# A three-layer kernel: seven block products for eight in the last layer's first matmul, a variance moved to ScalarE, and a new order of the last stage

## The chip, the cores and the metric

The kernel runs on one core of one Trainium2 chip. The metric is the device time of one execution, in microseconds (us). TensorE (PE in the profile; PEld is its weight load), VectorE (DVE), ScalarE (ACT), GpSimd (POOL) and SyncE (SP, which issues nearly all DMAs) run side by side. Each works through its own instructions strictly in order, and waits on semaphores for the others.

## The reference, cut to what matters

Attention with a decay feeds a feed-forward layer, and that feeds a second layer with a softmax gate and a layer norm. The change lies in the second layer, so this is the part to know:

```python
# 4 batches x 576 positions = 2304 tokens, 8 heads x 64 = 512 channels
x = attention(q, k, v, f)                        # (2304, 512)
y = leaky_relu(x @ w_in) @ w_out                 # first layer, 512 -> 2048 -> 512
h = y @ w2_in                                    # second layer's first product, 512 -> 1024
e = exp(h - max(h)); sm = e / (sum(e) + 1e-9)    # per token
s = h * sm
ln = (s - mean(s)) / sqrt(var(s) + 1e-6) * g_ln
out = ln @ w2_out                                # second layer's second product, 1024 -> 512
```

## The kernel before, in words

**Numbers.** Every float32 operand of a large product is scaled by a power of two and split into a high and a low float16 half. A product is then three float16 matmuls, high by high, high by low and low by high, summed in PSUM. `split` does this for a weight tile (`copy_f` writes the high half, `sub_f` the low one), `load_y` for the first layer's result. The scale comes from the largest value of the block: `bound` takes row maxima, and `power` sends them through a small float32 matmul against `ident` to spread the maximum over the partitions. That small matmul stands in PE's queue like any other.

**Stages.** Attention and the first layer (`ffn`: units of one 256-token block by one half of the hidden width) are interleaved until about 413 us. Then come the rest of the `ffn` units, and from 563 us the second layer. The 2304 tokens are 9 blocks of 256, taken in the order of the table `ORDER`. `load_y` reads a block of the first layer's result back from DRAM and splits it. A block is two tiles of 128 tokens, and `layer2` works on one tile.

**One tile of the second layer.** PE makes h: 128 tokens by 1024 columns in one of two PSUM tiles `ph` of two banks, 24 matmuls of 512 columns (two halves by four slices of 128 channels by three). DVE takes the row maximum (line 1083) and scales it (1085). ACT makes the exponential and its row sum (1086). DVE takes the reciprocal (1089, 1091) and multiplies gate and h (1092), after which `ph` is free. DVE takes mean and variance (1097, 1098), POOL the reciprocal root (1103 to 1106), and DVE applies both (1109). The result is split again (`hl`, lines 475 and 487), a DMA transposes it into `tr`, and PE makes the output tile: 24 matmuls of 512 columns into a bank `ps_g` or `ps_f`. ACT moves it to `ot` (1129), and a DMA writes it out.

**What sets the order.** The program isn't written in the order in which it runs. Each step is handed to a planner, `Plan`, with an engine (or a choice of engines), an estimated duration, a priority and the buffers that it touches. `Plan.run` plays the steps through against these estimates and emits each as its engine and buffers come free; the order of the instructions on every engine is fixed there, when the kernel is built. `prio` is the order wanted (lower first), `copy_f` and `sub_f` leave the engine to the planner, and `heirs` passes a tile on to another use once its first one has ended. So the three banks `ps_f` of the first layer go to `ps_g` after the last `ffn` unit; until then `ps_g` is a single bank.

All matmuls are recorded under line 518, the line of their helper `mm`. The profile's other helper lines are 472 to 479 (copies), 483 to 487 (differences), 658 (row maxima), 676 to 681 (`power`) and 781 (`tensor_tensor_reduce`, which adds two tensors and takes a row maximum or minimum in one instruction; here in attention).

Of the kernel before, what the change touches and what calls it, by code (L numbers as in the profile page):

```python
# [10 lines left out]
I32 = mybir.dt.int32  # L11
# [19 lines left out]
ORDER = (0, 1, 4, 5, 3, 2, 6, 8, 7)  # L31
# [11 lines left out]
EP = 1367.16  # L43
# [16 lines left out]
NWY = 19  # L60
NY2 = 4
NHL2 = 1
# [3 lines left out]
YB_ENGS = ("ACT",)  # L66
# [10 lines left out]
US0 = 20.0  # L77
HST = 2.59
# [41 lines left out]
WEIGHT2 = {"DVE": 0.71}  # L120
# [13 lines left out]
LO_ENGS = ("DVE", "POOL")  # L134

# [264 lines left out]
def body(tc, kqa, kq, vt, f, wa, w2i, w2o, gln, out):  # L400
# [80 lines left out]
    def sub_on(eng, o, a, b, scale=None):  # L481
# [5 lines left out]
        (nc.vector if eng == DVE else nc.gpsimd).tensor_tensor(o, a, b, op=ALU.subtract)  # L487
# [13 lines left out]
    def sub_f(o, a, b, n, prio, engs=(DVE, POOL), scale=None, psum=False, **kw):  # L501
        d = {DVE: dve(n) + (60 if scale else 0), POOL: pool2(n) + (pool1(n) + 40 if scale else 0)}
        return flex(engs, [d[e] for e in engs], lambda e: sub_on(e, o(), a(), b(), scale and scale()), prio, lock=not psum, **kw)
# [101 lines left out]
    attn_ops, XB = [], {}  # L605
# [347 lines left out]
    def split_w2i(prio):  # L953
        power(EI, 2 * KD + 1, [(EX, ("i2", j)) for j in range(2 * KD)], EW, "w2", prio, "ps_g")
        inverse(IW, ev(EW), "v2", "w2", prio)
        for h in range(2):
            for k in range(KD):
                W2I[k, h] = P.buf("wz")
                split(ZI[2 * k + h], W2I[k, h], lambda: ev(IW), [(EX, "v2")], prio + 0.3 * k + h)

    def load_w2o(c, prio):
        z, q = whole(w2o[c], prio), P.buf("wz")
        copy_f(lambda: q.t, lambda: z.t, 512, prio, scale=lambda: glt[:, c:c + 1], w=[q], r=[z])
        ZQ[c] = q
        sums(q, EQ + c, prio)
# [79 lines left out]
    def load_y(blk, prio):  # L1045
        yws, ys = [], []
        for q in range(2):
            yw = P.buf("yw")
            load(yw, lambda yw=yw: yw.t.rearrange("p (a n) -> p a n", a=2), lambda q=q: yp_d[blk][:, 2 * q:2 * q + 2], 128 * 512 * 4, prio, deps=YPD[blk][q:q + 1])
            bound(lambda yw=yw: yw.t, 512, EY + 3 * blk + q, ("y2", blk, q), prio, YB_ENGS, r=[yw])  # L1050
            yws.append(yw)
        power(EY + 3 * blk, 3, [(EX, ("y2", blk, q)) for q in range(2)], EE + blk, ("e", blk), prio, "ps_g")
        inverse(IY + blk, ev(EE + blk), ("iy", blk), ("e", blk), prio)
        P.op(DVE, 140, lambda: nc.vector.tensor_scalar(ev(SY + blk), ev(EE + blk), ev(EW), 2.0 ** (-2 * TOP), op0=ALU.mult, op1=ALU.mult), prio,
# [3 lines left out]
        for yw in yws:  # L1058
            y = P.buf("y2")
            copy_f(lambda y=y: y.t[:, 0], lambda yw=yw: yw.t, 512, prio, scale=lambda: ev(IY + blk), w=[(y, 0)], r=[yw, (EX, ("iy", blk))])  # L1060
            sub_f(lambda y=y: y.t[:, 1], lambda yw=yw: yw.t, lambda y=y: y.t[:, 0], 512, prio, scale=lambda: ev(IY + blk), w=[(y, 1)], rw=[yw], r=[(y, 0), (EX, ("iy", blk))])
            ys.append(y)
        return ys

    def layer2(tb, e, ys, prio, oprio):
        tt = 2 * tb + e
        eprio = prio - 5000
        ps, Eb, st, blk = P.buf("ph"), P.buf("raw2"), P.buf("s2"), ORDER[tb]
        E = lambda a=0, b=1024: Eb.t[:, a:b]
# [12 lines left out]
        P.op(PE, 24 * mmr(512), pe, prio, w=[ps], r=ys + list(W2I.values()))
        P.op(DVE, dve(1024), lambda: nc.vector.tensor_reduce(st.t[:, 0:1], ps.t, axis=AX.X, op=ALU.max, negate=True), eprio,
             w=[(st, 0)], r=[ps])
        P.op(DVE, 140, lambda: nc.vector.tensor_scalar(st.t[:, 0:1], st.t[:, 0:1], ev(SY + blk), None, op0=ALU.mult), eprio, rw=[(st, 0)], r=[(EX, ("s", blk))])  # L1085
# [7 lines left out]
            E(), E(), st.t[:, 3:4], ps.t, op0=ALU.mult, op1=ALU.mult), eprio, rw=[Eb], r=[ps, (st, 3)])  # L1093

        def stats():
            for h in range(2):
                nc.vector.bn_stats(st.t[:, 8 + 6 * h:14 + 6 * h], E(512 * h, 512 * h + 512))
            nc.vector.bn_aggr(st.t[:, 4:6], st.t[:, 8:20].rearrange("p (a b) -> p a b", a=2))  # L1098

        P.op(DVE, 2 * dve(512) + 40, stats, eprio, w=[(st, 4)], r=[Eb])  # L1100

        def rstd():
            nc.gpsimd.tensor_scalar(st.t[:, 5:6], st.t[:, 5:6], 1.0e-6, 1.0, op0=ALU.add, op1=ALU.mult)  # L1103
            nc.gpsimd.tensor_tensor(st.t[:, 6:7], st.t[:, 5:6], halfm, op=ALU.pow)
# [33 lines left out]
    with tc.manual_schedule():  # L1138
# [29 lines left out]
        def phase2():  # L1168
# [6 lines left out]
            P.tag("y2", tiles(bp, "y2", NY2, [128, 2, 512], F16))  # L1175
# [3 lines left out]
            P.tag("s2", tiles(bp, "s2", 3, [128, 20], F32))  # L1179
# [65 lines left out]
```

## Time and profile before

| what | us |
|---|---|
| median of 3 runs (764.88 to 766.02) | 764.99 |
| the profiled execution | 766.24 |
| its span, from the first to the last instruction | 764.5 |
| PE busy | 708.8 (93%) |
| DVE busy | 523.3 (68%) |
| ACT busy | 453.9 (59%) |
| POOL busy | 282.0 (37%) |

The profile is one execution. Its page gives busy time by engine, a digit row by slice of the span, and groups of like instructions; the trace behind it also gives the chain of work that ended last, waits, busy times by stretch, and the instructions in order of time. A matmul's own duration (379 ns for 512 columns) overlaps that of the next one, so the pace of PE is read from the starts of a row of matmuls. The profiled execution took 766.24 us, 1.25 us above the median, and 1.74 us of it lie outside the span.

### The profile page before, as it was taken

To read this page: it belongs to the slowest core of one execution; us is meant where nothing else is said; L and a number is where in the kernel's file an instruction comes from. 1 tells how busy PE (TensorE), PEld (TensorE's weight loads), DVE (VectorE), ACT (ScalarE), POOL (GpSimd) and SP (SyncE) were. 2 spreads that over 40 slices of the span, in tenths; PEclk is the share of its full clock that TensorE was granted. 3 is DMA by queue.
4 is the path that set the end of the run, shared out by engine and by line. 5 is a ranking of instruction groups with operands and counts; after the bars stand their busy time and mean duration, and the time that the engine had idled before them with its cause. 6 is when DMAs were issued, how large, how long until landed. Compare 5 with 4: busy or idle time off the path is not lost.

```text
span 764.5 us, 15462 instructions
## 1 busy us (share of the span) xinstructions
PE 708.8 (93%) x5657; PEld 538.6 (70%) x5657; DVE 523.3 (68%) x1329; ACT 453.9 (59%) x1109; POOL 282.0 (37%) x404
## 2 busy tenths in 40 slices
PE   0468799999999999999999999999999999999998
PEld 0346588898888888888889888888875444444443
DVE  5998788966977887777875575211226899677761
ACT  2699999976999689799984565122221332232121
POOL 4567878974365158565621132000000221111110
PEclk9999999999999999999999999999999999999999
DMA  8988479555657766768855640000003445343433
GB/s 225 309 236 220 113 229 222 128 108 122 159 109 151 132 141 147 118 135 153 177 120 118 215 137 4 17 13 15 15 1 83 98 111 116 91 111 82 84 83 82
DMA packets 163900, 94.17 MB, mean 123 GB/s; under 512 B 144224, under 2 KB 144240, under 8 KB 163824
## 3 DMA queue, kind: packets, MB, share of 16 engines
q1 hardware_dynamic: 163792, 93.17, 51.4%
q8 instruction: 44, 0.72, 0.4%
q14 instruction: 32, 0.26, 0.1%
q10 hardware_dynamic: 32, 0.02, 0.0%
HBM read 47.95 MB, written 10.06 MB: 76 GB/s over the span
## 4 chain that ended last, share of the span: by engine, by line
PE 53%; DMA 4%; ACT 2%; DVE 1%; issue 0%; POOL 0%; ACTq 0%; DVEq 0%; POOLq 0%
PE ps_f L518 32%; PE ph L518 12%; PE ps_g L518 4%; PE ps_s L518 3%; PE ps_v L518 2%; DMA raw<-w2o 1%; DMA raw<-w2i 1%; DMA pt<-hl 1%; DMA raw<-yp_d 1%; DVE wy L890 0%; DVE wy L483 0%; ACT wy L472 0%; ACT wk L472 0%; ACT ps_f L991 0%; ACT junk L906 0%
## 5 line engine op out<-in xcount | busy, mean ns | idle before, releaser
L518 PEld LDWEIGHTS <-wz 128*128 128x128 f16 x2700 | 262.0, 98 | 38.8 <-issue 7.0
L518 PE MATMUL ps_f<-g,wz 128*128 128x256 f16 x936 | 115.3, 275 | 0.2 <-DVE g L992 0.2
L518 PE MATMUL ph<-wy,y 128*128 128x512 f16 x432 | 95.8, 379 | 0.0
L483 DVE SCALAR_TENSOR_TENSOR hl<-ps_s,st,hl 128x512 f16<-128x512 f32 (+4 forms) x160 | 81.8, 539 | 16.7 <-ACT hl L472 14.9
L728 ACT ACTIVATE ps_s<-ps_s,st 128x512 f32<-128x512 f32 (+4 forms) x160 | 78.7, 492 | 17.8 <-DVE st L781 15.1
L1103 POOL TENSOR_SCALAR s<-s 128x1 f32<-128x1 f32 x18 | 3.9, 216 | 229.9 <-DVE s L1098 206.7
L472 ACT ACTIVATE hl<-ps_s,st 128x512 f16<-128x512 f32 (+4 forms) x155 | 76.0, 528 | 9.1 <-DVE st L749 2.7
L487 POOL TENSOR_TENSOR kq<-raw,kq 64x576 fp32r<-64x576 f32 x64 | 78.0, 1223 | 9.0 <-ACT kq L472 4.6
L518 PEld LDWEIGHTS <-qa 128*128 128x128 f16 x756 | 72.8, 98 | 10.2 <-issue 2.1
L518 PEld LDWEIGHTS <-tr 128*128 128x128 f16 x432 | 42.0, 98 | 50.6
L518 PEld LDWEIGHTS <-y 128*128 128x128 f16 x432 | 42.0, 98 | 50.1
L518 PE MATMUL ps_f<-dec,wz 128*128 128x256 f16 x576 | 72.0, 273 | 0.7 <-DVE g L992 0.7
L518 PE MATMUL ps_v<-pt,VT 128*128 128x128 f16 (+1 forms) x928 | 60.3, 216 | 13.2 <-DVE xr L815 9.8
L781 DVE CUSTOM_DVE_ANT_0 ps_s<-ps_s,mask 128x512 f32<-128x512 f32 (+3 forms) x128 | 62.6, 495 | 13.6 <-PE ps_s L518 12.7
L1086 ACT ACTIVATE raw<-ph,s,ex 128x1024 f32<-128x1024 f32 x18 | 21.6, 1203 | 81.6 <-DVE s L1085 75.9
L518 PEld LDWEIGHTS <-VT 128*128 128x128 f16 x928 | 53.0, 101 | 20.4 <-issue 9.4
L518 PE MATMUL ps_f<-x,wz 128*128 128x256 f16 x528 | 65.7, 277 | 0.0
L518 PE MATMUL ps_s<-kq 128*128 128x512 f32 (+5 forms) x256 | 62.0, 369 | 1.4 <-DVE hl L483 0.7
L992 DVE TENSOR_TENSOR g<-ps_f,g 128x512 f16<-128x512 f32 x42 | 28.9, 688 | 36.8 <-ACT ps_f L991 36.5
L518 PE MATMUL ps_f<-wy,tr 128*128 128x512 f16 x216 | 50.2, 379 | 0.0
L992 DVE TENSOR_TENSOR dec<-ps_f,dec 128x512 f16<-128x512 f32 x30 | 20.7, 689 | 37.7 <-ACT ps_f L991 37.5
L518 PEld LDWEIGHTS ps_s<-kq 128*128 128x128 f32 (+1 forms) x256 | 41.0, 192 | 6.6 <-DVE hl L483 1.2
(178 smaller groups left out, 1249.3 us busy)
## 6 DMA issues: line engine op xcount, KB each, us to landing
wst<-wa SPq DMA_DIRECT2D x32, 512.0 KB
raw<-kq SPq DMA_DIRECT2D x16, 480.0 KB
VT<-vt SPq DMA_DIRECT2D x16, 320.0 KB
raw<-yp_d SPq DMA_DIRECT2D x18, 256.0 KB
raw<-w2i SPq DMA_DIRECT2D x8, 512.0 KB
raw<-w2o SPq DMA_DIRECT2D x8, 512.0 KB
out<-ot SPq DMA_DIRECT2D x16, 256.0 KB
raw<-kqa SPq DMA_DIRECT2D x12, 256.0 KB
```

The source lines that it names most:

```text
L472: nc.scalar.activation(o, i, CP, scale=1.0 if scale is None else scale)
L483: nc.vector.scalar_tensor_tensor(o, a, scale, b, op0=ALU.mult, op1=ALU.subtract)
L487: (nc.vector if eng == DVE else nc.gpsimd).tensor_tensor(o, a, b, op=ALU.subtract)
L518: nc.tensor.matmul(o, lhsT=l, rhs=r, start=start, stop=stop)
L728: P.op(ACT, act(W, 1, True) + 93, lambda view=view, j=j, k=k: nc.scalar.activation(view(), view(), AF.Exp, bias=sts.t[:, j:j + 1], scale=- ...
L781: P.op(DVE, dve(W) + 130, lambda i=i, j=j, view=view: nc.vector.tensor_tensor_reduce(view(), view(), mask[:, 512 - 128 * i:640], -0.125, 3 ...
L992: P.op(DVE, dve(512) + 60, lambda: nc.vector.tensor_tensor(g.t[:, 1], ps.t, g.t[:, 0], op=ALU.subtract), eprio, w=[(g, 1)], r=[ps, (g, 0)])
L1086: P.op(ACT, act(1024, 2, True), lambda: nc.scalar.activation(E(), ps.t, AF.Exp, bias=st.t[:, 0:1], scale=ev(SY + blk), accum_out=st.t[:, 1 ...
L1103: nc.gpsimd.tensor_scalar(st.t[:, 5:6], st.t[:, 5:6], 1.0e-6, 1.0, op0=ALU.add, op1=ALU.mult)
```

## The change

**Strassen's scheme.** h of one block (256 tokens by 512 channels, times 512 by 1024) is seen as a 2 by 2 product of blocks: two token tiles, two halves of the channels, two halves of the columns. `layer2` now takes a whole block. Instead of eight block products it makes seven, in Winograd's form with shared sums, on sums and differences of the operands. One block product is 6 matmuls of 512 columns (`prod`). Products 0, 2 and 5 go to single banks (`g1`, `g6`, `g7`), the others straight into the banks of the block's two `ph` tiles.

- `split_w2i` makes four differences of weight tiles for each of two channel slices, and splits 14 weight tiles where there were 8.
- `load_y` makes four sums and differences of y (256 columns each), and splits 1792 columns a block where there were 1024. The row maxima move from ACT to DVE (`YB_ENGS`).
- `layer2` puts the products together: ACT copies `g1` to SBUF, DVE makes three sums (`plus`) and four `tensor_tensor_reduce` (`full`), which also give the row maximum. The `tensor_reduce` of line 1083 goes.

**The variance.** `bn_stats` and `bn_aggr` on DVE go. The multiplication of gate and h now also gives the row sum, DVE scales it to the negative mean, and ACT makes a squaring pass with a row sum. The last scale and shift may go to DVE or ACT (`N_ENGS`).

**Order and buffers.** `L2P`, `OUTP` and `LYP` are tables of priorities, and blocks 0 to 3 of the second layer now stand among the last `ffn` units. There are two `hl2` buffers for one, four `s2` for three, two larger `y2`, new tiles `sy`, `rr` and `wide`, and `ORDER`, `EP`, `US0`, `HST` and `YD` have other values, which also moves some `ffn` units and attention steps against each other from about 130 us on.

The core of the diff:

```diff
-ORDER = (0, 1, 4, 5, 3, 2, 6, 8, 7)
+ORDER = (0, 1, 4, 5, 3, 2, 8, 6, 7)
-EP = 1367.16
+EP = 1307.15
-NHL2 = 1
+NHL2 = 2
-YB_ENGS = ("ACT",)
+YB_ENGS = ("DVE",)
+L2P = (1300.0, 1366.2, 1370.0, 1390.0, 1410.0, 1430.0, 1450.0, 1470.0, 1476.09)
...
     def split_w2i(prio):
-        for h in range(2):
-            for k in range(KD):
-                W2I[k, h] = P.buf("wz")
-                split(ZI[2 * k + h], W2I[k, h], lambda: ev(IW), [(EX, "v2")], prio + 0.3 * k + h)
+        for k in range(2):
+            b11, b12, b21, b22 = (ZI[2 * (k + 2 * q) + h] for q in range(2) for h in range(2))
+            t3, t2, t4 = (P.buf("wz") for _ in range(3))
+            sub_f(V(t3), V(b22), V(b12), 512, prio + k, w=[t3], r=[b22, b12])
+            sub_f(V(b12), V(b12), V(b11), 512, prio + k, rw=[b12], r=[b11])
+            sub_f(V(t2), V(b22), V(b12), 512, prio + k, w=[t2], r=[b22, b12])
+            sub_f(V(t4), V(b21), V(t2), 512, prio + k, w=[t4], r=[b21, t2])
+            for n, z in enumerate((b11, b12, t2, b21, b22, t3, t4)):
+                W2I[k, n] = P.buf("wz")
+                split(z, W2I[k, n], lambda: ev(IW), [(EX, "v2")], prio + k + 0.1 * n)
...
+    def layer2(tb, y, prio, oprios):
+        p1, p2, blk = P.buf("ph"), P.buf("ph"), ORDER[tb]
+        g1, g6, g7 = P.buf("ps_g"), P.buf("ps_g"), P.buf("ps_g")
+        a11, a12, x1, a22, x3, x2, x4 = ROWS
+        def prod(p, at, n, pr):
+            def pe():
+                for k in range(2):
+                    yh, yl = (y.t[:, j, at + 128 * k:at + 128 * k + 128] for j in range(2))
+                    wh, wl = (W(W2I[k, n], j) for j in range(2))
+                    mm(bank(p)(), yh, wh, k == 0, False)
+                    mm(bank(p)(), yh, wl, False, False)
+                    mm(bank(p)(), yl, wh, False, k == 1)
+        prod(g1, a11, 0, prio)
+        prod(g6, x2, 2, prio + 0.1)
+        prod((p1, 0), a12, 3, prio + 0.2)
+        prod(g7, x3, 5, prio + 0.3)
+        prod((p2, 1), x1, 1, prio + 0.4)
+        prod((p1, 1), x4, 4, prio + 0.5)
+        prod((p2, 0), a22, 6, prio + 0.6)
+        P.op(ACT, act(512, 0, True), lambda: nc.scalar.activation(r1.t, g1.t, CP), eprio, w=[r1], r=[g1])
+        plus(u2, g6, r1, w=[u2], r=[g6, r1])
+        full((p1, 0), r1, s1, 0)
+        plus(u3, g7, u2, w=[u3], r=[g7, u2])
+        plus(u2, (p2, 1), u2, rw=[u2], r=[(p2, 1)])
+        full((p2, 1), u3, s2, 0)
+        full((p1, 1), u2, s1, 1)
+        full((p2, 0), u3, s2, 1)
+        for e, (p, st) in enumerate(((p1, s1), (p2, s2))):
+            normal(2 * tb + e, blk, p, st, eprio, oprios[e])
...
-        P.op(DVE, 2 * dve(512) + 40, stats, eprio, w=[(st, 4)], r=[Eb])
+        P.op(ACT, act(1024, 2), lambda: nc.scalar.activation(
+            wide[0], E(), AF.Square, bias=st.t[:, 4:5], accum_out=st.t[:, 5:6]), eprio, w=[(st, 5)], r=[Eb, (st, 4)])
```

**How PE's queue changes.** The first place is one block in the steady part of the second layer, on PE. `ph0` and `ph1` are h, `y` the split block, `tr` the transposed gate result of an earlier tile, `ps_g0` and `ps_f` single banks, and the row with `ident` is the small matmul of `power`, which waits for a DVE row maximum (`va`). Before, one tile, then `power`, then an output and the next tile (the first row of each run of like ones):

```order
L518 MATMUL ph0_5622<-wy11_5636,y22_5646 128x512
...
L518 MATMUL ps_f2_168<-ident_115,va1_119 128x128
...
L518 MATMUL ps_f0_166<-wy4_5629,tr0_5649 128x512
...
L518 MATMUL ph1_5623<-wy11_5636,y22_5646 128x512
...
L518 MATMUL ps_g0_5624<-wy4_5629,tr1_5650 128x512
```

Now, block 5:

```order
L524 MATMUL ps_g0_5554<-wy9_5564,y21_5570 128x512
...
L524 MATMUL ps_f1_167<-wy11_5566,y21_5570 128x512
...
L524 MATMUL ph0_5552<-wy12_5567,y21_5570 128x512
...
L524 MATMUL ps_f0_166<-wz7_70,y21_5570 128x512
...
L524 MATMUL ps_f2_168<-ident_115,va1_119 128x128
...
L524 MATMUL ps_g0_5554<-wz3_66,tr1_5576 128x512
...
L524 MATMUL ph1_5553<-wy10_5565,y21_5570 128x512
...
L524 MATMUL ph0_5552<-wy13_5568,y21_5570 128x512
...
L524 MATMUL ph1_5553<-wst1_99,y21_5570 128x512
```

What moved: a run of 24 matmuls into one `ph` tile has become seven runs of 6 for two tiles, three of them into single banks that DVE and ACT must empty, and `power` stands between the fourth and the fifth.

The second place is the end of DVE's queue. `ph`, `s` and `raw` belong to a tile, `hl` is its split result. Before, the last tile but one ends, and the last one begins:

```order
L1109 TENSOR_SCALAR raw1_91<-raw1_91,s21_5655 128x1024
L475 CAST hl20_5648<-raw1_91 128x1024
L487 TENSOR_TENSOR hl20_5648<-raw1_91,hl20_5648 128x1024
L1083 TENSOR_REDUCE s22_5656<-ph1_5623 128x1
L1085 TENSOR_SCALAR s22_5656<-s22_5656,ex_116 128x1
```

Now, block 7 (tiles 14 and 15) ends, and block 8 (tiles 16 and 17) begins:

```order
L1155 TENSOR_SCALAR raw0_90<-raw0_90,s22_5582 128x1024
L481 CAST hl20_5573<-raw0_90 128x1024
L493 TENSOR_TENSOR hl20_5573<-raw0_90,hl20_5573 128x1024
L493 TENSOR_TENSOR hl21_5574<-raw1_91,hl21_5574 128x1024
L1108 ISA ph0_5552,s20_5580<-ph0_5552,wst1_99 128x512
...
L1104 TENSOR_TENSOR sd2_95<-ph1_5553,sd2_95 128x512
```

What moved: tile 15's low half (`hl21` from `raw1`, whose scale, shift and high half ACT now makes) stands ahead of all of the last block's merges.

## Rows read from the trace of the kernel before

**Rows 1.** The page: busy time by engine, and digit rows of PE and its clock.
```profile
PE 708.8 (93%) x5657; PEld 538.6 (70%) x5657; DVE 523.3 (68%) x1329; ACT 453.9 (59%) x1109; POOL 282.0 (37%) x404
PE   0468799999999999999999999999999999999998
PEclk9999999999999999999999999999999999999999
```

**Rows 2.** Busy us by stretch: PE, PEld, DVE, ACT, POOL; granted clock, DMA share, GB/s.
```profile
200.00:300.00 100.00, 97.89 (x943) 85.23 (x941) 80.91 (x247) 86.68 (x237) 46.85 (x69) 1.00 0.65 135
300.00:400.00 100.00, 99.37 (x1010) 87.53 (x1009) 75.62 (x228) 90.28 (x231) 55.72 (x75) 1.00 0.73 142
450.00:500.00 50.00, 49.71 (x455) 44.34 (x454) 20.00 (x32) 20.85 (x40) 6.21 (x6) 1.00 0.16 53
600.00:650.00 50.00, 50.00 (x235) 22.84 (x234) 47.10 (x90) 15.64 (x30) 10.75 (x27) 1.00 0.48 113
700.00:764.50 64.50, 60.68 (x282) 27.30 (x279) 34.78 (x55) 12.18 (x19) 6.01 (x20) 0.99 0.39 86
```

**Rows 3.** The chain that ended last, its end: start us, us, what.
```profile
463.70 99.58 PE ps_f L518 x912
563.28 5.18 PE ph L518 x24
...
729.60 5.18 PE ph L518 x24
...
745.14 15.55 PE ps_f L518 x72
...
760.76 0.69 ACT ot L1129
```

**Rows 4.** What PE waited for after 380 us: us in total, times, longest.
```profile
PE ps_g L518 <- DVE va L658: 0.9, 2, 0.6
```

**Rows 5.** The last tile on DVE, ACT and POOL: start us, us, engine, line.
```profile
727.41 1.22 DVE L1083 TENSOR_REDUCE s<-ph 128x1 f32<-128x1024 f32 x1
737.90 1.22 DVE L1083 TENSOR_REDUCE s<-ph 128x1 f32<-128x1024 f32 x1
739.46 1.21 ACT L1086 ACTIVATE raw<-ph,s,ex 128x1024 f32<-128x1024 f32 x1 [8.62 <-DVE s L1085]
741.24 1.28 DVE L1092 SCALAR_TENSOR_TENSOR raw<-raw,s,ph 128x1024 f32<-128x1024 f32 x1
742.55 1.29 DVE L1097 BATCH_NORM_STATS2 s<-raw 128x6 f32<-128x512 f32 x2
744.17 0.19 POOL L1103 TENSOR_SCALAR s<-s 128x1 f32<-128x1 f32 x1 [9.02 <-DVE s L1098]
745.67 0.81 DVE L1109 TENSOR_SCALAR raw<-raw,s 128x1024 f32<-128x1024 f32 x1 [1.59 <-POOL s L1106]
746.52 0.69 DVE L475 CAST hl<-raw 128x1024 f16<-128x1024 f32 x1
747.25 1.22 DVE L487 TENSOR_TENSOR hl<-raw,hl 128x1024 f16<-128x1024 f32 x1
```

**Rows 6.** DVE groups with shapes kept apart: count, busy us, mean ns.
```profile
L781 DVE CUSTOM_DVE_ANT_0 ps_s<-ps_s,mask 128x512 f32<-128x512 f32 x32 | 22.4, 700 | 8.2 <-PE ps_s L518 8.2
L992 DVE TENSOR_TENSOR dec<-ps_f,dec 128x512 f16<-128x512 f32 x30 | 20.7, 689 | 37.7 <-ACT ps_f L991 37.5
L781 DVE DVE_READ_ACCUMULATOR2_ANT st<- 128x1 f32 x128 | 17.8, 139 | 0.1
L483 DVE SCALAR_TENSOR_TENSOR y<-raw,ex,y 128x512 f16<-128x512 f32 x18 | 12.7, 746 | 0.0
L483 DVE SCALAR_TENSOR_TENSOR wy<-wy,ex,wy 128x512 f16<-128x512 f32 x9 | 7.9, 930 | 0.0
```

**Rows 7.** As rows 2, where the last tile's transposing DMA ends.
```profile
753.50:754.00 0.50, 0.50 (x4) 0.20 (x2) 0.00 (x0) 0.00 (x0) 0.00 (x0) 1.00 0.94 217
754.00:754.50 0.50, 0.50 (x4) 0.22 (x3) 0.00 (x0) 0.00 (x0) 0.00 (x0) 1.00 0.22 53
```

More of the change, by code (lines that the diff above doesn't have):

```diff
@@ L76 @@
 NGT = 4
[L77 to L78 removed]
+US0 = 21.76
+HST = 2.56
 TB = 256
@@ L119 @@
 WEIGHT = {"DVE": 7.06}
-WEIGHT2 = {"DVE": 0.71}
+WEIGHT2 = {"DVE": 1.06}
 HEAT = 0.25
@@ L134 @@
 LO_ENGS = ("DVE", "POOL")
+S_ENGS = ("DVE", "POOL")
+N_ENGS = ("DVE", "ACT")
 class Plan:
@@ L499, in copy_f, with sub_f @@
         return flex(engs, [d[e] for e in engs], lambda e: copy_on(e, o(), i(), scale and scale()), prio, lock=not psum, **kw)
-    def sub_f(o, a, b, n, prio, engs=(DVE, POOL), scale=None, psum=False, **kw):
+    def sub_f(o, a, b, n, prio, engs=(DVE, POOL), scale=None, psum=False, op=ALU.subtract, **kw):
         d = {DVE: dve(n) + (60 if scale else 0), POOL: pool2(n) + (pool1(n) + 40 if scale else 0)}
-        return flex(engs, [d[e] for e in engs], lambda e: sub_on(e, o(), a(), b(), scale and scale()), prio, lock=not psum, **kw)
+        return flex(engs, [d[e] for e in engs], lambda e: sub_on(e, o(), a(), b(), scale and scale(), op), prio, lock=not psum, **kw)
     queue = {SP: nc.sync, ACT: nc.scalar, POOL: nc.gpsimd}
@@ new lines, in load_y @@
+        pieces = [(512 * e, 512, lambda e=e: four(yw.t[:, 0:1024])[:, e::2], (yw, "e%d" % e)) for e in range(2)] + [(1024, 768, lambda: four(sy.t), sy)]
+        for at, n, v, k in pieces:
+            copy_f(lambda at=at, n=n: four(y.t[:, 0, at:at + n]), v, n, prio, scale=lambda: ev(IY + blk), w=[(y, (0, at))], r=[k, (EX, ("iy", blk))])
+        for at, n, v, k in pieces:
+            sub_f(lambda at=at, n=n: four(y.t[:, 1, at:at + n]), v, lambda at=at, n=n: four(y.t[:, 0, at:at + n]), n, prio, scale=lambda: ev(IY + blk),
+                  w=[(y, (1, at))], rw=[k], r=[(y, (0, at)), (EX, ("iy", blk))])
@@ L1174, in phase2 @@
             P.tag("wz", tiles(bp, "wy", NWY, [128, 512], F32))
-            P.tag("y2", tiles(bp, "y2", NY2, [128, 2, 512], F16))
+            P.tag("y2", tiles(bp, "y2", NY2, [128, 2, 1792], F16))
+            wide.append(bp.tile([128, DF2], BF16, name="wide"))
+            P.tag("sy", tiles(bp, "sy", 1, [128, 768], F32))
             P.tag("hl2", tiles(bp, "hl2", NHL2, [128, 2048], F16))
@@ L1189, in body @@
         split_w2o(950.0)
-        for n in ("ps_f", "ps_g", "yo", "wst", "raw", "raw2", "wk", "wz", "g", "x", "VT", "va"):
+        for n in ("ps_f", "ps_g", "yo", "wst", "raw", "raw2", "wk", "wz", "g", "x", "VT", "va", "rr", "y2"):
             P.tags.setdefault(n, Tag(n)).fifo = False
-        heirs("raw", "raw2", "raw2", lambda t: [("yw", v) for v in halves(t, F32)])
+        heirs("raw", "raw2", "raw2", lambda t: [("yw", t)])
+        flat = lambda t: t.rearrange("p j n -> p (j n)").bitcast(F32)
+        heirs("x", *[lambda t: [("wz", flat(t))]] * 3, *[lambda t: [("rr", flat(t))]] * 3, *[lambda t: [("wz", flat(t))]] * 4)
         heirs("ps_f", "ps_g", "ps_g", "ps_g")
         for tb in range(NB):
-            ys = load_y(ORDER[tb], 2000.0 + 4 * tb - 5000)
-            for e in range(2):
-                layer2(tb, e, ys, 2000.0 + 10 * (2 * tb + e), 2000.0 + 10 * (2 * tb + e) + OLAG)
+            ys = load_y(ORDER[tb], LYP + 4 * tb)
+            layer2(tb, ys, L2P[tb], [OUTP[tb] + 10 * e for e in range(2)])
         P.run()
```

111 lines of the change are left out of this document (55 added, 56 removed).

## The prediction

> **What bounds the kernel now.** I read the page first: PE is busy 708.8 of 764.5 us, its digit row reads 9 from the sixth slice to the last but one, and the granted clock is 1.00, the 2.4 GHz level [rows 1]. A share is only an average, so the table by stretch came next. PE's idle time is 2.1 us in 200:300, 0.6 in 300:400, 0.3 in 450:500 and none in 600:650; what it misses in 700:764.5 is the end, where the output leaves [rows 2]. The chain of what ended last says the same: from 463.7 us to 760.7 it is PE alone, one run of matmuls after another, and then 0.69 us of ACT and the last DMA [rows 3]. So PE's own work sets the end, and a removed matmul is time gained as long as no other engine becomes late.
>
> The second engine to look at is DVE. It is busy 20 of 50 us in 450:500, but 47.1 of 50 in 600:650 [rows 2], and in the last tiles its row maximum comes every 10.49 us (727.41, 737.90) [rows 5] where PE makes a tile in 2 x 5.18 = 10.36 us [rows 3]. So in the second layer DVE already runs at PE's pace, with nothing to spare. That is where a gain can get lost.
>
> **The removed matmuls.** 24 matmuls of 512 columns take 5.18 us [rows 3], 0.216 us each. 18 tiles x 24 = 432 become 9 blocks x 7 x 6 = 378, so 54 go: **-11.65 us**. All stood on the path. From the first of the new products to the end PE's queue holds 810 matmuls of 512 columns, 864 of 256 (912 take 99.58 us, 0.109 each [rows 3]) and seven small ones (0.33): 175 + 94 + 2 = 271.5 us. That puts the first new product at about 478 us, where the kernel before has DVE mostly idle.
>
> On this price a rule of the Trainium skill differs from the row. TensorE: Matmul & The Clock Gate, Back-to-back issue gap, gives about 131 ns for a 512-column matmul in a sustained stream of weight loads and matmuls. By that the 54 would be worth 7.1 us. The chain's 5.18 us for 24 speak against it.
>
> **DVE's work for a block.** Per block, two tiles: the four merges cost 0.70 + 0.14 each and the three sums 0.69 [rows 6], 5.4 us. The products of gate and h cost 2 x 1.28, two low halves 2 x 1.22, one scale and shift 0.81 and one high half 0.69 (the other two go to ACT) [rows 5]: 6.5 us. Eight small steps at about 0.2 (two of them fill the 0.57 us between the accumulated sum and 741.24 [rows 5]) are 1.6. The block's y takes two row maxima (0.69 by the like-sized sums), three low halves at 0.75, 0.75 and about 1.0 [rows 6], one high half and one sum (about 1.0 together) and `power`'s five small steps (1.1): 6.0. With 0.035 us between instructions (727.41 + 10.49 shows no more where DVE doesn't wait), 38 of them, it is 20.8 us. What goes is 2 x 1.22 and 2 x (1.29 + 0.2) [rows 5]. So DVE carries 20.8 us a block as against 21.0 before, while PE needs 42 x 0.216 + 2 x 5.18 + 0.33 = 19.8. **PE has become quicker than DVE**; that works only because the blocks are no longer done one after another at this pace. Counting the order's instructions between one and the same merge of successive blocks, DVE has 41, 22, 23 and 21 us of work up to block 4 and PE 80, 26, 30 and 26, since `ffn` units stand between; then DVE has 20.0, 20.9, 17.0 and 14.4 (the last blocks prepare no y), PE 19.8, 19.8, 14.3 and 19.4. Summed over blocks 4 to 8 that is 72 us against 73: DVE doesn't fall far behind, if it seldom waits.
>
> **Where PE will wait.** Three places.
> *power.* Its small matmul stands in PE's queue behind a DVE maximum. In block 5 PE reaches it 1.3 + 5.18 + 4 x 1.3 = 11.7 us after the merge's product of block 4. DVE, by its order, needs 12.1: the two last merges, low halves of y, both products of gate and h, two maxima that wait for a load, one sum. I take **+0.5** (before, the longest such wait was 0.6 [rows 4]); the ends are 0, and 3 if the load and ACT's part are late. For the other blocks I find 0.3 to 7 us to spare.
> *The single bank.* Among the `ffn` units `ps_g` is one bank. Products, `power` and outputs use it 21 times in blocks 0 to 3, often with only one product, 1.3 us, between. Emptying takes 0.69 on DVE [rows 6] or ACT [rows 3], which leaves 0.6. I find one place, behind `power` of block 3, where DVE has a scale and shift and a high half ahead of it: **+0.5**, with ends 0 and the rival below.
> *The end.* Before, the last tile's low half ended at 748.47 [rows 5], and its transposing DMA and the output issued behind it were through by 754.2 [rows 7]; for `tr` I take 5.0 us after the low half. Its matmuls began only at 745.14 + 10.36 = 755.5 [rows 3]. Now three outputs, 15.5 us, stand between the last product and tile 16's output. But tile 15's low half stands ahead of the last merges in DVE's queue, and waits for ACT's square, POOL's root, ACT's scale and shift and its high half; by my walk its product of gate and h ends 6.5 us before the last product does, then come 0.2 for the mean, 1.3 for the square, 1.5 for the root, two ACT passes of about 1.1 (a little under the exponential's 1.21) and 1.22, with 0.5 of hand-overs: it ends 0.4 us after the last product. Then follow, from the rows, four merges less one and a sum (3.2), scale (0.2), exponential (1.4), two small steps (0.4), product (1.28), mean (0.2), square (1.4, by the exponential's row), root (1.5: 744.17 to 745.67 [rows 5]), scale and shift, high half and low half (2.7), hand-overs (0.9) and 5.0 of DMA: 18.6. 18.6 - 15.5 = **+3.1**. Without the block ahead the merges would run as their products come and nothing would be waited for, so the ends are 0 and about 4.
>
> **At nothing.** ACT gains two squares and a copy, some 3.4 us a block, with 15.6 of 50 us busy in 600:650 [rows 2]; POOL likewise (10.8). The eight differences and six more splits of weights give DVE up to 8 x 0.69 + 6 x 0.93 = 11 us [rows 6] before 478, where it has 30 of 50 free; gone, that cover would delay the first product, but `ffn` units stand ahead. The new order from 130 us on may move PE's idle time by 1 us either way. What SP issues is the same count of DMAs.
>
> **Sum.** 766.24 - 11.65 + 0.5 + 0.5 + 3.1 = 758.7 for an execution like the profiled one. That one is 1.25 above the median, so **757.4**.
>
> **The rivals.**
> *DVE becomes the bound* (14%). If its two-source instructions run at 0.93 instead of 0.746, as they do in the weight stage [rows 6], DVE's 72 us for blocks 4 to 8 become 83 against PE's 73; with some 3 us of slack PE loses 7 more: 761 to 764. For it: 47.1 of 50 busy, and only 0.2 us a block saved. Against: the split of y, beside POOL's work too, ran at 0.746. The Trainium skill has such a mechanism (SBUF — State Buffer, SBUF: two separate sides): DVE instructions with two SBUF inputs and GpSimd's reads lock each other out of one pair of ports. The trace agrees only in the weight stage's 0.93.
> *The single bank makes it slower* (10%). PE's queue is in order, so each of the 21 uses of `ps_g` that isn't emptied in time stops all of PE. A DVE product (1.28) or low half (1.22) ahead of the emptying step [rows 5] uses up the 0.6 us left and 0.7 more; at 0.7 to 0.8 each it is 16 us: about 769. It decides from 11.65 / 21 = 0.55 us a use. Against: with `ffn` units between, DVE has half its time free there.
> *A matmul is worth less* (3%): 131 ns as by the page, 7.1 us gained, 762.
> *The gain is eaten* (5%): waits of 10 to 13 us spread over `power`, attention's new order and the end: 764 to 766.
> My forecast, PE bound with 0 to 9 us of waiting, 753 to 762, has 68%.
>
> **Chances and range.** Below 0.2% (1.5 us, about what a measurement of this kernel can tell) is no change. Faster: 68 + 10 (most of the DVE case) + 3 = 81%; same: 4 + 5 = 9%; slower: 10%. The range goes from all waits at nothing and 1 us won in the order, 764.99 - 11.65 - 1 = 752.3, to 763, into the DVE case: that leaves out less than 2 in 10.
>
> **What would show it.** Right: 378 matmuls where 432 were, 24 still in 5.18 us; PE busy near 697; PE's waits below 6 us after 478 us, one of some 3 us ahead of tile 16's output, on a DMA. DVE-bound: DVE near 50 of 50 in 630:740 and PE waiting in every block for a DVE product of gate and h or a maximum. Single bank: many waits of about 0.7 us on `ps_g` before 640. Wrong altogether: a new wait in attention, or a first product well after 478.

## The result, and the profile after

The changed kernel takes 755.27 us (median of 4 runs, 753.55 to 756.95) beside 764.93 for the kernel before (763.07 to 766.02): a ratio of 0.9876, interval 0.9841 to 0.9911. A second comparison with more runs gave 0.9878 (0.9856 to 0.9901). So some 9.7 us are gained where 7.6 were forecast, and 755.27 lies inside the range. One execution in the experiments, 1222.7 us of the first kernel of experiment 9, ran at a mean granted clock of 0.58 and is left out of that kernel's median.

The profiled execution took 756.95 us. Its page, against [rows 1]:

```profile
span 755.2 us, 15580 instructions
PE 698.0 (92%) x5603; PEld 533.8 (71%) x5603; DVE 535.7 (71%) x1420; ACT 502.6 (67%) x1160; POOL 324.3 (43%) x439
```

PE has 54 instructions and 10.8 us of work less; DVE, ACT and POOL have more of both. PE's idle time is 57.2 us, before it was 55.7: of the 10.8 us 1.5 are lost again, and the span is 9.3 us shorter. The table by stretch stands against [rows 2]. Its columns are PE, PEld, DVE, ACT and POOL busy, the granted clock, the DMA share and GB/s:

```profile
600.00:650.00 50.00, 49.85 (x309) 29.98 (x307) 34.81 (x80) 21.50 (x34) 10.35 (x21) 1.00 0.38 90
650.00:700.00 50.00, 49.85 (x233) 22.65 (x232) 41.53 (x99) 26.50 (x38) 14.14 (x27) 1.00 0.34 85
700.00:755.20 55.20, 50.18 (x231) 22.32 (x229) 27.25 (x56) 22.71 (x33) 9.53 (x22) 0.99 0.43 96
```

DVE's 47.1 of 50 us are gone; its fullest stretch of 50 behind 450 us has 41.5. The chain that ended last, against [rows 3], has the first new product and the end:

```profile
478.96 1.29 PE ps_g L524 x6
...
722.60 2.87 PE ph L524 x12
725.48 5.18 PE ps_g L524 x24
730.65 15.54 PE ps_f L524 x72
746.20 5.19 PE ps_g L524 x24
```

After the last product PE makes its five outputs without a gap: the wait that was forecast ahead of tile 16's output (behind 15.5 us of outputs, at 741.0) isn't there. What PE waited for behind 440 us, the whole list, against [rows 4]:

```profile
PE ph L524 <- DVE sd L1104: 1.4, 2, 1.2
```

A note on reading times. Single executions of one kernel differ by several us (the kernel before ran from 759.3 to 768.1 in one series), so medians alone tell 2 us only roughly. The traces tell more. I take the stretch from the start of the first new product to the end of PE's last matmul: 478.80 to 751.39, **272.6 us** in the changed kernel, and 478.69 to 751.30, 272.6 again, in a second execution. What differs between executions lies ahead of it: the same product started at 472.71 in one experiment below.

And a note on reading stops. A matmul's own 379 ns outlast the pace of 216, so the first 0.16 us of a stop of PE still count as busy, and the lists of waits leave short stops out. Read from start to start instead, PE has seven stops between the first new product and the end in the changed kernel, from 0.06 to 1.33 us and 2.7 us in all, each of them ahead of a product into `ph`; the list gives 1.4 of it. (That is also about what PE's busy time, 10.8 us less, lacks to 54 times 0.216, 11.65.)

### The profile page after: what moved, and what is told of

The parts are those of the page before. It is cut to its first block, busy times and chain, and to the rows that moved or that the text cites. A ratio compares the mean times of both kernels' runs of the same rounds, so it can differ in the third digit from the quotient of the medians.

```text
span 755.2 us, 15580 instructions
## 1 busy us (share of the span) xinstructions
PE 698.0 (92%) x5603; PEld 533.8 (71%) x5603; DVE 535.7 (71%) x1420; ACT 502.6 (67%) x1160; POOL 324.3 (43%) x439
## 4 chain that ended last, share of the span: by engine, by line
PE 70%; ACT 9%; DVE 5%; DMA 3%; issue 2%; POOL 1%; SPq 0%; ACTq 0%; POOLq 0%; DVEq 0%
PE ps_f L524 47%; PE ps_g L524 8%; PE ps_s L524 6%; PE ph L524 5%; PE ps_v L524 4%; DMA wst<-wa 2%; ACT ps_s L734 2%; ACT hl L478 1%; DVE hl L489 1%; ACT xr L818 1%; ACT kq L478 1%; DVE VT L489 1%; ACT ps_f L1003 1%; DMA pt<-hl 1%; ACT wz L478 1%
## 5 line engine op out<-in xcount | busy, mean ns | idle before, releaser
L524 PE MATMUL ps_f<-g,wz 128*128 128x256 f16 x828 | 104.8, 276 | 0.2 <-DVE g L1004 0.2
L524 PE MATMUL ps_f<-dec,wz 128*128 128x256 f16 x684 | 84.5, 273 | 0.0
L524 PEld LDWEIGHTS <-y 128*128 128x128 f16 x378 | 36.6, 98 | 45.6 <-issue 3.7
L787 DVE CUSTOM_DVE_ANT_0 ps_s<-ps_s,mask 128x128 f32<-128x128 f32 (+3 forms) x128 | 62.3, 494 | 7.6 <-PE ps_s L524 6.2
L524 PE MATMUL ps_f<-sd,wz 128*128 128x256 f16 x330 | 45.0, 273 | 0.0
L821 DVE SCALAR_TENSOR_TENSOR xr<-ps_v,xr 64x256 f32<-64x256 f32 (+1 forms) x96 | 33.9, 353 | 15.3 <-ACT xr L818 13.9
L1003 ACT ACTIVATE ps_f<-ps_f 128x512 f32<-128x512 f32 x72 | 42.5, 590 | 0.3
L524 PE MATMUL ps_f<-wst,wz 128*128 128x256 f16 x330 | 42.3, 273 | 0.0
```

Of the source, the lines that this page charges most:

```text
L524: nc.tensor.matmul(o, lhsT=l, rhs=r, start=start, stop=stop)
L787: P.op(DVE, dve(W) + 130, lambda i=i, j=j, view=view: nc.vector.tensor_tensor_reduce(view(), view(), mask[:, 512 - 128 * i:640], -0.125, 3 ...
L821: P.op(DVE, dve(n) + 60, lambda: nc.vector.scalar_tensor_tensor(xr.t[a:a + 64, dst0:dst0 + n], ps.t[a:a + 64, c0:c1], PS, xr.t[a:a + 64, d ...
L1003: P.op(ACT, act(512, 0, True), lambda: nc.scalar.activation(ps.t, ps.t, AF.Prelu, scale=GS, alpha=0.01), eprio, rw=[ps])
```

## The experiments

In experiments 3, 4, 5, 7 and 8 the edit changes only what a step emits, and the order of the steps stays as it was; in 2, 6 and 9 the planner makes a new order from the values shown.

**1. The changed kernel again.**

> The changed kernel once more, unedited, to have it beside the kernel before and the other experiments on one chip. Both theories on the gain: 753 to 757, ratio 0.985 to 0.991. In the trace the stretch from the first new product's start to PE's last matmul should be 272.4 us again, within 0.5, and what differs between executions should lie before it.

755.10 us beside 764.24, ratio 0.9878 (0.9856 to 0.9901), the stretch 272.6. Up to 450 us PE got through the same work before and after. The row of that stretch of the kernel before:

```profile
0.00:450.00 450.00, 398.41 (x3660) 343.27 (x3661) 351.10 (x1025) 365.67 (x946) 250.22 (x323) 1.00 0.69 162
```

And of the changed kernel (398.67 in its second execution):

```profile
0.00:450.00 450.00, 398.33 (x3659) 343.61 (x3660) 359.18 (x1037) 372.46 (x950) 261.38 (x330) 1.00 0.69 160
```

**2. The new order alone, in the kernel before.**

```diff
-ORDER = (0, 1, 4, 5, 3, 2, 6, 8, 7)
+ORDER = (0, 1, 4, 5, 3, 2, 8, 6, 7)
```

(and `EP`, `US0`, `HST`, `YD` likewise).

> The kernel before with the changed kernel's values of ORDER, EP, US0, HST and YD alone: attention and feed-forward units in the new order, the second layer as it was. Theory A, the new order gives or takes nothing of note and the removed matmuls are the whole gain: 763 to 766 beside 764, PE's idle time before 450 us at 50 to 53. Theory B, part of the gain comes from the order: 760 to 762, PE's idle time before 450 us below 50.

763.32 beside 764.24, ratio 0.9990 (0.9968 to 1.0012). PE's idle time before 450 us was 50.0 (450 less 399.96), 1.6 less than before, but this tells little: two executions of one and the same order, in the changed kernel and in experiment 3, have 51.7 and 46.2. By the interval the order is worth 2.4 us at most, so it isn't where most of the 9.7 us come from.

**3. The 54 matmuls put back.**

```diff
-P.op(PE, 6 * mmr(512), pe, pr, ...
+twice = lambda: (pe(), pe())
+P.op(PE, 6 * mmr(512), twice if p is g1 else pe, pr, ...
```

> The changed kernel with the same order on every engine, but product 0 of each block is issued twice (the second pass begins the sum anew), so that PE has the 54 matmuls of 512 columns back and nothing else differs. Theory A, PE sets the end and a removed matmul is worth 0.216 us: 755.3 + 54 x 0.216 = 767.0, within 1. Theory B, the gain comes from the order and the earlier start of the blocks, and PE had spare time behind other engines: 755.3 + less than 6 = 756 to 761. Theory C, a matmul in a stream is worth 0.131: 762.4.

764.73 beside 763.89, ratio 1.0013 (0.9985 to 1.0041): the gain is gone with the matmuls. (The median is 2.3 below theory A's 767; but beside the kernel before in its own series it is 0.8 slower, where the changed kernel was 9.7 faster, 10.5 apart.) From the first new product to the end, the changed kernel's row:

```profile
478.80:760.00 281.20, 270.87 (x1683) 164.37 (x1680) 166.05 (x367) 115.53 (x177) 57.39 (x104) 0.99 0.28 68
```

And this one's:

```profile
472.71:760.00 287.29, 282.54 (x1737) 169.60 (x1734) 165.98 (x367) 115.66 (x177) 57.47 (x104) 1.00 0.27 67
```

54 records more and 11.67 us more of PE: 0.216 each, as [rows 3] had it, and not 0.131 (7.1 us). The stretch grew by 10.6; the other 1.0 us came out of stops, which are 1.7 us from start to start where the changed kernel has 2.7. Theory A stands; B and C fall.

**4. Fewer matmuls than the change leaves: where does DVE take over?**

```diff
 mm(bank(p)(), yh, wh, k == 0, False)
-mm(bank(p)(), yh, wl, False, False)
-mm(bank(p)(), yl, wh, False, k == 1)
+mm(bank(p)(), yh, wl, False, k == 1)
```

> The changed kernel with the same order on every engine, but each block product leaves out its low by high matmuls: 4 matmuls for 6, 126 fewer in all. The products are then less exact, everything else is done. It shows where DVE takes over as the bound. Theory A with DVE at the 20.8 us a block of the prediction: 126 x 0.216 = 27.2 go from PE, but in blocks 4 to 8 PE's 73 us become 58 against DVE's 72, of which 3 are slack: 728 + 11 = 739. Theory A with DVE's instructions overlapping (about 18.5 us a block): 58 against 63, 728 + 2 to 5 = 730 to 733. PE alone everywhere: 728. DVE already bound now: above 748.

741.08 beside 763.89, ratio 0.9701 (0.9643 to 0.9759). The stretch shrank by 15.1 us only, to 257.5, though 27.2 us of matmuls went. The two largest of PE's waits behind 440 us:

```profile
PE ph L524 <- DVE sd L1103: 4.3, 3, 3.3
PE ph L524 <- DVE s L1107: 4.1, 6, 1.7
```

And the stretch that ends with the longest of them, and the one behind it (columns as above, the clock third from the end):

```profile
680.00:689.00 9.00, 5.44 (x25) 2.28 (x24) 6.61 (x15) 5.38 (x8) 2.39 (x8) 1.00 0.08 30
689.00:693.00 4.00, 3.97 (x12) 1.47 (x12) 4.00 (x7) 0.60 (x1) 0.00 (x0) 0.64 0.44 85
```

All waits come to 10.1 us, and PE's busy time fell by 23.5 and not by 27.2. Of these 3.7 us 1.7 are matmuls behind the longest stop, at a lower granted clock (0.64 on average in 689:693; ten from 689.89 to 693.74 took 3.85 us where 2.16 is the pace), and most of the rest is the first 0.16 us of each of the added stops. So a second saving, of this size, would be worth a little over half. The time is nearest the one that went with DVE at 20.8 us a block (739), but DVE isn't full: 6.61 of 9.00 us where PE waits most, with 2.35 us of waiting for POOL's root ahead of the sum that PE needs. It is late at single places there, not out of time.

**5. The variance, back on DVE in the changed kernel, and moved alone in the kernel before.** The edit of the first, in short (`stats` holds the two `bn_stats` and `bn_aggr`):

```diff
-P.op(DVE, 70, lambda: nc.vector.tensor_scalar(st.t[:, 4:5], st.t[:, 4:5], -1.0 / DF2, ...
+P.op(DVE, 70, stats, eprio, rw=[(st, 4)], r=[Eb])
-P.op(ACT, act(1024, 2), lambda: nc.scalar.activation(wide[0], E(), AF.Square, ...
+P.op(ACT, act(1024, 2), lambda: None, ...
```

> The changed kernel with the same order on every engine, but mean and variance are made by bn_stats and bn_aggr on DVE again; ACT makes no squares, and the product of gate and h gives no row sum. DVE gains 2 x (1.29 + 0.2) and loses 2 x (0.2 + 0.14) a block: +2.3. Theory A, DVE's 20.8 us a block stand without slack beside PE's 19.8: in blocks 4 to 8 5 x 2.3 = 11.5 less 3 of slack, so 763 to 764. Theory B, DVE has about 2 us a block to spare: 755 to 757, the move of the variance buys next to nothing here.

> The kernel before, with the variance on ScalarE alone: the product of gate and h gives the row sum, DVE scales it, ACT makes the squaring pass, and bn_stats and bn_aggr go; the order is kept. Theory A, PE sets the end there too, and DVE's relief of 2 x (1.29 - 0.14) us a block goes nowhere: 763 to 765, ratio within 0.2% of 1. Theory B, DVE held PE up in the second layer: 758 to 761, since DVE was busy 47.1 of 50 us there.

In the changed kernel 759.18 beside 763.89, ratio 0.9938 (0.9908 to 0.9968), and the stretch took 277.0 us, 4.4 more. In the kernel before, 764.52 beside 763.96, ratio 1.0001 (0.9979 to 1.0024): nothing, although DVE fell from 37.2 to 32.2 busy us in 650:700 there. PE's list in the former:

```profile
PE ph L524 <- DVE s L1108: 2.1, 3, 1.3
PE ps_f L524 <- DVE va L664: 1.5, 2, 1.0
PE ph L524 <- DVE sd L1104: 1.1, 2, 0.9
...
```

The merges, and the maximum ahead of `power` (`va`), are late now. So the same edit is worth nothing without the new products and 4.4 us with them, in the order that was made for the variance on ACT (an order made anew for DVE wasn't tried). Both theories of the first were off: with no slack it would have been 8, with 2 us a block to spare nothing; in the kernel before theory A's 763 to 765 came.

**6. All blocks behind the last feed-forward unit.** Here the planner makes a new order.

```diff
-L2P = (1300.0, 1366.2, ... 1476.09)
+L2P = tuple(2000.0 + 20 * n for n in range(9))
-OUTP = (1340.0, 1370.0, ... 1520.0)
+OUTP = tuple(2040.32 + 20 * n for n in range(9))
```

> The changed kernel, but the tables of priorities are set so that all blocks of the second layer come behind the last feed-forward units, one after another, as in the kernel before (the planner orders the steps anew from there). Theory A, as predicted, the early blocks are needed because DVE at 20.8 us a block is slower than PE at 19.8: 9 x 1 = 9 us more, and some 2 for the first block's start, 764 to 767. Theory B, DVE keeps up at about 18.5 us a block and only the count of matmuls matters: 755 to 758.

763.86 beside 763.89, ratio 1.0003 (0.9979 to 1.0027): the whole gain is lost. The number is 0.1 us from theory A's 764 to 767, the reason mostly another. PE's waits:

```profile
PE ps_g L524 <- DMA tr<-hl: 5.9, 1, 5.9
PE ph L524 <- DVE s L1108: 1.9, 3, 0.9
PE ph L524 <- DVE sd L1104: 1.1, 1, 1.1
```

5.9 us are one wait: with no `ffn` unit left to do, PE stands until the first transposed tile is there, and the 15 matmuls behind it took 2.2 us longer than the pace (598.09 to 603.53), at a lower granted clock. Lateness on DVE is 3.0 us over all nine blocks, not the 9 that a pace of 20.8 against 19.8 would have brought. So the early blocks are needed, above all to cover the start.

**7. The end: tile 15's low half made longer.**

```diff
+if tt == 15:
+    lo.emit = lambda one=lo.emit: [one() for _ in range(4)]
```

> The changed kernel with the same order, but tile 15's low half is made four times on DVE, so that it ends 3 x 1.22 = 3.7 us later and the last block's merges behind it start where the prediction had them, at the last product's end. Theory A, the term of the end was right in its mechanism and only the walk on DVE was too late: the merges then end some 3.2 us later, tile 16's low half at about 737.3 instead of 734.1, and PE waits 1 to 3 us for tile 16's transpose: 756 to 758 where the changed kernel has 755, and a wait on a DMA ahead of tile 16's output. Theory B, the end has more room than that: no wait, 755.

759.29 beside 764.24, ratio 0.9928 (0.9907 to 0.9950), some 4 us above the changed kernel; the stretch took 278.0 us, 5.4 more. Neither theory's number came (756 to 758, 755), and PE didn't wait for a DMA. Its rows of this kernel, in order of time, and then DVE's:

```profile
716.38 2.75 PE L524 MATMUL ph<-wy,y 128*128 128x512 f16 x12
722.95 0.82 PE L524 MATMUL ph<-wy,y 128*128 128x512 f16 x3 [3.81 <-DVE s L1108]
723.59 1.46 PE L524 MATMUL ph<-sd,y 128*128 128x512 f16 x3
724.84 1.49 PE L524 MATMUL ph<-wst,y 128*128 128x512 f16 x3
...
717.23 5.00 DVE L493 TENSOR_TENSOR hl<-raw,hl 128x1024 f16<-128x1024 f32 x4 [2.81 <-ACT hl L478]
722.14 0.69 DVE L1108 CUSTOM_DVE_ANT_0 ph<-ph,wst 128x512 f32<-128x512 f32 x1
722.75 0.14 DVE L1108 DVE_READ_ACCUMULATOR2_ANT s<- 128x1 f32 x1
```

And the clock right behind:

```profile
724.00:725.00 1.00, 1.00 (x4) 0.44 (x3) 0.10 (x2) 0.00 (x0) 0.00 (x0) 0.50 1.12 214
```

PE had made products into the first half of one `ph` tile and the second half of the other, and stood before the next, into the other half of the first tile. It started at 722.95, when the merge that DVE had just ended (722.14, its accumulator at 722.75 to 722.89) was the one of the half made before. The halves are different banks, but one tile, and the product waits for the tile's reader. (Two separate tiles weren't tried, since the exponential reads both halves in one instruction.) Then three matmuls took 1.25 us (723.59 to 724.84) where 0.65 is the pace, at a granted clock of 0.50, the 1.2 GHz level. 3.8 us of stop and 1.6 us of slower matmuls (PE's busy time in the stretch: 272.45 against 270.87) make the 5.4. A merge late by 3.7 us costs this where it stands, not at the end.

**8. The single bank emptied later.**

```diff
-P.op(DVE, dve(512) + 60, lambda: nc.vector.tensor_tensor(o.t, bank(p)(), b.t, op=ALU.add), ...
+P.op(DVE, dve(512) + 60, lambda: [one() for _ in range(2 if tb < 4 and p in (g6, g7) else 1)], ...
-P.op(ACT, act(512, 0, True), lambda: nc.scalar.activation(r1.t, g1.t, CP), ...
+P.op(ACT, act(512, 0, True), lambda: [out1() for _ in range(2 if tb < 4 else 1)], ...
```

> The changed kernel with the same order, but in blocks 0 to 3, where the products share one bank, each of the three steps that empty it (a copy on ACT, two sums on DVE) is made twice: 12 emptyings, 0.69 us later each. Theory A, the 1.3 us of the product between leave 0.6: each adjacent use waits 0.1 to 0.3, +1 to +3 us in all, 756 to 758. Theory B, the bank has no room left (the rival's mechanism): 12 x 0.69 = +8.3, 763. Theory C, the bank has ample room: 755.

757.95 beside 764.24, ratio 0.9898 (0.9871 to 0.9926); the stretch took 275.3 us, 2.7 more where 8.3 were added. PE's list for 478 to 640 us has three waits of 0.2 us on the bank:

```profile
PE ph L524 <- DVE sd L1104: 0.9, 1, 0.9
PE ps_g L524 <- DVE sd L1104: 0.6, 3, 0.2
```

From start to start it is more: seven uses of the bank stop PE for 0.18 to 0.38 us, 2.0 us in all, and the stop on `ph` in block 0 grows by 0.7 (from 0.38 to 1.10), which makes the 2.7. So this is theory A. Where the bank is tightest it has 0.3 to 0.5 us of room a use, a little less than the 0.6 counted; the changed kernel itself shows no stop on it.

**9. The last two products exchanged.** A product that follows one into the same tile needs no merge in between. So the two into `p2` are put side by side:

```diff
-prod((p1, 1), x4, 4, prio + 0.5)
-prod((p2, 0), a22, 6, prio + 0.6)
+prod((p2, 0), a22, 6, prio + 0.5)
+prod((p1, 1), x4, 4, prio + 0.6)
```

Once with the merges, tiles and outputs exchanged as well, once without.

> The changed kernel with the last two products of each block exchanged, and the merges, the tiles and their outputs with them: the two products into tile p2 now follow each other, so that no product starts 1.3 us behind one whose other half DVE is still to read. Theory A, the 1.4 us that PE waits for DVE in block 7 and block 0 come from the two halves of one tile sharing their dependence: the stretch from the first new product to PE's last matmul takes 271.0 to 271.6 us instead of 272.4, the time 754.0 to 754.8. Theory B, DVE is late by itself and PE waits as long at the next merge: 272.4, 755.

> As the run before it, but only the two products are exchanged on PE, and the merges, tiles and outputs keep their order. Theory A: the wait goes as well, but the first tile's exponential starts one product later, 271.0 to 272.0 for the stretch. Theory B: 272.4 or more, because tile 16's output is reached sooner than its transposed input lands.

752.56 and 752.87 beside 763.96, ratios 0.9856 (0.9825 to 0.9887) and 0.9857 (0.9833 to 0.9882): both faster than either kernel by the median, the first also than theory A's 754.0 to 754.8. The first one's trace is of the execution that was left out, so the second's is read. There the stretch took 271.5 us (474.60 to 746.07), 1.1 less than in the changed kernel and within theory A's 271.0 to 272.0, and the wait on DVE is gone from PE's list:

```profile
PE ps_f L524 <- ACT ot L1178: 0.8, 1, 0.8
PE ps_f L524 <- DMA tr<-hl: 0.5, 1, 0.5
```

What is left are two waits that were covered before: an output's bank that ACT hasn't emptied, and a transposed tile. From start to start they are 1.6 us (0.94 and 0.66) and the only stops, where the changed kernel has its 2.7, all ahead of products into `ph`: that is the 1.1. (The planner made a new order around the exchange, so the two new stops may be that order's.) Of the 2.2 us between the medians the traces account for 1.1. The intervals of the ratios overlap with 0.9878's, so the rest may be chance.

## Why the prediction was right, and where it wasn't

**The removed matmuls: right.** 54 times 0.216 is 11.65 us, and experiment 3 put 11.67 us of PE work back with them and lost the whole gain. PE bounds the kernel before and after. The work of PE's queue from the first new product was put at 271.5 us and measured 270.9, and the product came at 478.8 for "about 478".

**The waits of `power` and of the single bank: too high, and small.** 0.5 us each was set down, and neither has an entry in PE's list. The ends given (0) hold. The rival of the bank needed 0.55 us a use; with 0.69 more for each of twelve emptyings PE stopped on it for 2.0 us (experiment 8).

**DVE's work for a block: mis-sized.** 20.8 us was the sum of 38 durations with 0.035 us between them. Between two like products (the starts of those behind the small waits in blocks 4 and 5, 19.80 us apart, the whole of a steady block) DVE has this:

```profile
649.30:669.10 19.80, 16.46 (x40) 1.00 0.37 89
```

A block is 39 instructions (the stretch cuts into two of the like merge at its ends and counts both). Their durations add up to 18.98 us, near the sum, which has 19.5 without its gaps, but their union is 16.46: an instruction that doesn't need its predecessor's result begins about 0.08 us before that one ends. One sees it in these rows of the changed kernel:

```profile
711.91 0.21 DVE L1136 TENSOR_SCALAR s<-s,ex 128x1 f32<-128x1 f32 x1
712.04 0.14 DVE L1142 TENSOR_SCALAR s<-s 128x1 f32<-128x1 f32 x1
712.16 0.16 DVE L1138 RECIPROCAL s<-s 128x1 f32<-128x1 f32 x1
712.36 1.28 DVE L1139 SCALAR_TENSOR_TENSOR raw<-raw,s,ph 128x1024 f32<-128x1024 f32 x1
713.56 0.08 DVE L1139 DVE_READ_ACCUMULATOR raw<-raw,s,ph 128x1 f32 x1
```

0.21 us from 711.91 would end at 712.12, but the next row starts at 712.04; only the product, which needs the reciprocal just made, starts behind its end (712.36 after 712.32). So DVE had 3.3 us to spare in a block, and "PE has become quicker than DVE" was wrong. "Nothing to spare" in the kernel before was wrong too: the row maximum every 10.49 us was PE's pace, and with DVE at 37.8 busy us in 600:650 where it had 47.1 (experiment 5) nothing was won. Experiment 6 shows it from another side (3.0 us of lateness in nine blocks, not 9), and experiment 4 fits: with 14 matmuls fewer a block PE needs 19.8 less 3.0, 16.8 us, next to DVE's 16.5, and there the waits begin. The DVE rival's 14% were thus too many for its reason. Its rate didn't come either: the 512-column low halves of y took 0.77 us, not 0.93.

**The end: wrong, in place and mechanism.** Of the +3.1 us nothing came. The step that failed is the walk of DVE up to tile 15. Its product of gate and h was to end 6.5 us before PE's last product; it ended 11.8 before (713.64 against 725.47); the overlaps above, 3.3 us a block, are enough to explain it. From there to the end of the low half the sum had 6.9 us, and 8.3 were needed. The rows of tile 15 on POOL, behind those of tile 14:

```profile
713.54 0.19 POOL L1147 TENSOR_SCALAR s<-s 128x1 f32<-128x1 f32 x1 [11.36 <-ACT wide L1143]
713.82 0.55 POOL L1148 TENSOR_TENSOR s<-s,halfm 128x1 f32<-128x1 f32 x1
714.45 0.19 POOL L1149 TENSOR_SCALAR s<-s 128x1 f32<-128x1 f32 x1
714.74 0.27 POOL L1150 TENSOR_SCALAR s<-s 128x1 f32<-128x1 f32 x1
715.25 0.65 POOL L1147 TENSOR_SCALAR s<-s 128x1 f32<-128x1 f32 x1 [0.24 <-ACT wide L1143]
715.99 1.00 POOL L1148 TENSOR_TENSOR s<-s,halfm 128x1 f32<-128x1 f32 x1
717.08 0.82 POOL L1149 TENSOR_SCALAR s<-s 128x1 f32<-128x1 f32 x1
718.00 0.27 POOL L1150 TENSOR_SCALAR s<-s 128x1 f32<-128x1 f32 x1
```

And DVE's at the same time:

```profile
715.04 0.81 DVE L1155 TENSOR_SCALAR raw<-raw,s 128x1024 f32<-128x1024 f32 x1 [1.21 <-POOL s L1150]
715.89 0.69 DVE L481 CAST hl<-raw 128x1024 f16<-128x1024 f32 x1
716.62 1.23 DVE L493 TENSOR_TENSOR hl<-raw,hl 128x1024 f16<-128x1024 f32 x1
```

The root took 1.5 us for tile 14 and 3.0 for tile 15, beside DVE's scale and shift, high half and low half of tile 14. Still the low half was done 3.6 us before the last product (721.89) and not 0.4 behind it, so the merges ran as the products came. And had the walk been right, the price would have been another: experiment 7 ends that low half at 722.23, 0.2 us behind where the last product would have ended without the stop, near the 0.4 of the walk, and PE then stops for 3.8 us before a product, because of the tile that two products share, and never comes to the wait on the transposed tile. This coupling was in none of the terms or rivals.

**What the sum left out.** That same coupling is PE's one listed wait, 1.2 us in block 7 and 0.2 in block 0. It is in the steady blocks too, unlisted: in block 4 the merge of one half of a tile ends at 649.25 (its accumulator's row), and the product into the other half, which the pace would have had at 648.99, starts at 649.30 (the row of the chain):

```profile
649.11 0.14 DVE L1108 DVE_READ_ACCUMULATOR2_ANT s<- 128x1 f32 x1
...
649.30 1.46 PE ph L524 x6
```

Block 5 has the same 0.31 us. In block 7 DVE had a scale and shift, which waited 0.9 us for POOL, and a high half ahead of the sum that PE waited for:

```profile
702.22 0.81 DVE L1155 TENSOR_SCALAR raw<-raw,s 128x1024 f32<-128x1024 f32 x1 [0.90 <-POOL s L1150]
702.95 0.69 DVE L481 CAST hl<-raw 128x1024 f16<-128x1024 f32 x1
703.55 0.68 DVE L1104 TENSOR_TENSOR sd<-ph,sd 128x512 f32<-128x512 f32 x1
...
704.29 0.81 PE L524 MATMUL ph<-wst,y 128*128 128x512 f16 x3 [1.17 <-DVE sd L1104]
```

In experiment 9 it is gone. Together: the forecast had 271.5 us of work and 4.1 of waits from the first new product on; it was 270.9 and 1.7. That is 3.0 us less. By that way of adding, with 478 for the start and 5.6 us behind PE's last matmul, the forecast would have been 759.2 for the profiled execution; 3.0 less and 0.8 more for the later start make the 756.95 that it took. (The sum in the prediction came to 758.7.) The median lies 2.1 below 757.4. So what carried the forecast is the 11.65 us. That its waits (4.1 us, in three places) and the stops found (2.7 from start to start, in a fourth) are of one size is luck, and the wrong price of DVE cost so little because the sum holds it only in the walks behind the terms of `power` and of the end.

**At nothing: right for the new order (experiment 2, as closely as it tells), not for the variance.** It was treated as a part of DVE's sum; it is worth 4.4 us here and nothing by itself (experiment 5).

## What to carry to other kernels

Price a removed instruction on the bounding engine by the starts of a row of like ones, and look for waits in the shape of the dependences, not only in sums: two products that write different halves of one tile wait for each other's readers, and the order of the products decides whether that shows. An engine's load is the union of its instructions and not the sum of their durations; 39 of them can look full at 83%. The same edit can be worth nothing before a change and several us behind it, so a part is judged in the kernel that it ends up in.

## What the runs showed of the hardware that was not expected

- **A long stop of PE costs more than the stop.** Behind the stop of 3.8 us in experiment 7 the granted clock was 0.81 in 723:724, 0.50 in 724:727 and 0.99 in 727:728; in experiment 6 it was 0.50 already in the last 2 us of the stop of 5.9 (596:598), and still in 598:602; behind the 3.3 us of experiment 4 it was 0.64 in 689:693. Stops of 1.2 us (the changed kernel) and 1.7 us (experiment 4, 672.56) left it at 1.00 in the rows. In experiment 7 this added 1.6 us to 3.8, in experiment 6 2.2 to 5.9.
- **POOL's small instructions grow beside DVE's.** The power of one column took 0.55 us in one tile and 1.00 in the next, and a scaling 0.19 and 0.82; each of the longer ones ended 0.05 to 0.4 us behind the end of a DVE instruction from SBUF to SBUF (715.85, 716.58 and 717.85). The Trainium skill (SBUF — State Buffer, SBUF: two separate sides) has DVE and GpSimd share one pair of ports that one of them holds for a whole instruction while the other is blocked, on DVE's side for instructions in a two-port mode or with two SBUF inputs. The scaling of 0.82 us beside the difference with two SBUF inputs (716.62) agrees with it; in which mode the other two DVE instructions ran, no run here shows. The prediction put a price on DVE's side alone.
